# A unit's row of maxima: one write, loads right behind it, and no extra maxima in the first four cycles of an attention kernel

## The chip, the cores and the metric

The kernel runs on one core of a Trainium2 chip. The metric is the device time of one execution in microseconds. Before the change three runs took 1613.4, 1613.86 and 1617.51 us: the median is 1613.86.

## What is computed

One block of a transformer with adaptive layer norm, in float32: 2048 tokens, width 512, 32 query heads of width 16 that share one key head and one value head, and a dense layer of width 1792 with ReLU.

```python
mod = (silu(c) @ w_mod).reshape(1, 6, 1, 512)
sa, ca, ga, sb, cb, gb = (mod[:, i] for i in range(6))
h = layernorm(x) * (1 + ca) + sa
q = (h @ wq).reshape(1, 2048, 32, 16).transpose(0, 2, 1, 3)
k, v = h @ wk, h @ wv
p = softmax(einsum("bhqd,bkd->bhqk", q, k) * 16 ** -0.5)
x = x + ga * (merge_heads(einsum("bhqk,bkd->bhqd", p, v)) @ wo)
h = layernorm(x) * (1 + cb) + sb
return x + gb * (relu(h @ w1) @ w2)
```

## The kernel before

**Units.** The attention is cut into 32 units: 8 blocks of 256 tokens times 4 groups of 8 heads. A unit has its queries in two tiles `qp`, four columns (`ct` 0 to 3) of 512 query rows each, two in the lower half of the partitions and two in the upper. Rows 0 to 47 of a half hold the queries, split in a high and a low part so that a product of rounded numbers keeps its precision; rows 48 and 49 hold minus the row maximum, high and low part, against rows of ones in the keys `kp`. So a score matmul (`scores`, TensorE, line 907) gives the score less its maximum, and the exponential (ScalarE, line 909) needs no further work. `values` (line 1084) multiplies the exponentials `pe` with the values into the bank `ps_pv`.

**Row of maxima.** Before that, `max_of` computes the same products (line 534, into one of three banks `ps_max`) and VectorE reduces each to its maxima (line 536), 64 times a unit. After the last, VectorE reduces once more (`negm`, line 540) and transposes (`sq`, line 496). `max_rows` returns two steps. `parts` splits `sq` into `ms`, high part on ScalarE (line 314), low part on GpSimd (line 315), and writes it to a scratch tensor `mdr` in DRAM. `load` reads `mdr` back as rows 48 and 49 of the unit's `qp`, in four loads, one for each `ct`. A write or load waits on its queue until what it needs is done, and what stands behind it in that queue waits too. For unit 0 both use SP's and ScalarE's queue, later only SP's.

**Cycles.** The main loop has 256 cycles, 8 for each unit. In a cycle go 8 score matmuls with their exponentials, 8 maxima of the next unit (a "place"), two groups of value matmuls, and a portion of other matmuls into the one bank `ps_fill`, the fill: query projections in cycles 0 to 32 and a few later ones, then the output projection and the dense layer of the block that is done. A string of letters sets the order in a cycle; there is one for each size of the portion. `a` and `b` are maxima, `c` and `d` scores, `u` and `l` fill matmuls on the upper and lower half of TensorE's rows, `V` the value matmuls, `P` the place where steps of ScalarE and GpSimd that were put off are issued. Work on the lower half of the rows runs beside work on the upper half, so the letters come in pairs.

```python
    6: "aucuaucPeuaucuasdVtbldlbldldelblbscV",
    3: "bcaucuuacdlbldlbVPbacddaV",
    "e": "aucuaucPeuaucuadVtbldlbldldelblbcV",
```

A portion of three matmuls has the order 3, which holds its maxima in pieces of five and three. The order 6 has four in each half. Portions of six, and the first ones in full float32, use it. The letter `e` is an extra maximum of a list `extra`. It holds the 8 maxima of one place, which go two to a cycle in the cycles 0 to 3. With the 16 maxima of unit 1 that are done before the loop, a unit's last maximum falls three places ahead: unit u's maxima end in cycle 8u - 4, and its first scores, which run one or two ahead of their cycle, stand late in cycle 8u - 1.

**The row in the loop.** Its `parts` goes to the end of the list `put_off` in cycle 8u - 3 and is issued at that cycle's `P`. Its `load` goes to `ends`, which is issued at the end of the same cycle. `put_off` also holds the splits of other tiles (`hh`, `r`, `w1s`, `qq`), and `to_dram`, three stores of 256 KB that bring a projected query tile to DRAM (`qdr`, line 429). `load_q` reads such a tile back for the next unit (line 480), 16 maxima before the unit's end. From cycle 13 on, with pauses, chores are issued at a cycle's end: loads of weights (`raw`, lines 862 and 873) and stores of their split form (`w1dr`, line 868). In the dense layer SP loads `w1s` (line 562), one tile of 512 KB a cycle.

Of the kernel before, what the change touches and what calls it, by code (L numbers as in the profile page):

```python
# [9 lines left out]
F32 = mybir.dt.float32  # L10
# [19 lines left out]
KB = S // 512  # L30
# [37 lines left out]
def build(tc, nc, cst, sb, ps, dr, x, wq, wk, wv, wo, w1, w2, c, w_mod, out):  # L68
# [244 lines left out]
    def split(hi, lo, src, eng=None):  # L313
        nc.scalar.activation(hi, src, AF.Copy)  # L314
        (eng or nc.gpsimd).tensor_tensor(lo, src, hi.bitcast(F32), op=OP.subtract)  # L315
# [4 lines left out]
    def split_psum(hi, lo, pt, func=AF.Copy, stg=None, **kw):  # L320
        stg = stage() if stg is None else stg
        nc.scalar.activation(stg, pt, func, **kw)  # L322

        def parts():
            split(hi, lo, stg)

        return parts


    put_off = []  # L330

    def add_psum(dst, pt, other):
        stg = stage()
# [84 lines left out]
    def qproj(b, j, bank, soon=False, tag=None, n0=0):  # L418


        pt = bank()
        todo = [("f32", pt[:, n:n + TB], wqf[j][:, k], hT[b][:, k, n:n + TB],
                 n + k == n0, n + k == TB + DC - 1)
                for n in range(n0, LB, TB) for k in range(DC)]

        def to_dram(qq):
            stored.add((b, j))
            for r, part in ((0, 0), (32, 0), (16, 1)):
                nc.sync.dma_start(qdr[b][j].bitcast(F32)[:, r:r + 16, n0:], qq[:, part, n0:].bitcast(F32))

        def end():
            qt = sb.tile([P, 2, LB], F32R, name="qq", tag=tag or "t4", bufs=3 if tag else 2)
            if soon:
                nc.scalar.activation(qt[:, 0, n0:], pt[:, n0:], AF.Copy, scale=DH ** -0.5)
                nc.vector.scalar_tensor_tensor(qt[:, 1, n0:], pt[:, n0:], DH ** -0.5,
                                               qt[:, 0, n0:].bitcast(F32),
                                               op0=OP.mult, op1=OP.subtract)
                to_dram(qt)
                return
            stg = sb.tile([P, 512], F32, name="stg", tag="tmp", bufs=2)  # L440
            put_off.append(split_psum(qt[:, 0, n0:], qt[:, 1, n0:], pt[:, n0:], stg=stg[:, n0:], scale=DH ** -0.5))
            put_off.append(partial(to_dram, qt))

        return todo, end

# [46 lines left out]
    def max_rows(u, negm):  # L492


        sq = sb.tile([P, 32], F32, name="sq", tag="sq", bufs=2)
        nc.vector.transpose(sq, negm)
        mdr = dr.tile([2, 16, 4, 32], F32, name="mdr", tag="mdr", bufs=4)

        def queue(n):
            return nc.scalar if u == 0 and n % 2 else nc.sync  # L500

        def parts():
            ms = sb.tile([P, 2, 32], F32R, name="ms", tag="ms", bufs=2)
            split(ms[:, 0], ms[:, 1], sq)
            for q in range(4):
                queue(q).dma_start(mdr[:, :, q].rearrange("p a n -> a p n"),
                                   ms[q * 32:q * 32 + 16].bitcast(F32))

        def load():
            for ct in range(4):  # L510
                r = (ct % 2) * 64 + 48
                queue(ct).dma_start(qps[u][ct // 2][r:r + 2].bitcast(F32),
                                    mdr[:, ct * 4:ct * 4 + 4].rearrange("p j q n -> p (j q n)"))

        return parts, load

# [27 lines left out]
    places = [(0, i, j) for i in range(2) for j in range(4)]  # L544
    first_max = [(0, hf, i, j, kb) for kb in range(KB) for _, i, j in places for hf in (1, 0)]
    places = [(u, i, j) for u in range(1, NU) for _, i, j in places]
    first_max += [(u, hf, i, j, kb) for u, i, j in places[:LEAD // 8]
                  for kb in range(KB) for hf in (1, 0)]
    places = places[LEAD // 8:]
    extra = [(*places[0][:1], hf, *places[0][1:], kb) for kb in range(KB) for hf in (1, 0)]  # L550
    places = places[1:]

# [485 lines left out]
    for what in HEAD:  # L1040
        if what == "q":
            q = firsts.pop(0)
# [25 lines left out]
    pvt, ends = None, []  # L1068
# [5 lines left out]
    def in_turn(steps):  # L1074
        for step in steps:
            step()
# [13 lines left out]
    for c in range(NU * KT // 2):  # L1090
# [4 lines left out]
        if places:  # L1095
            u, i, j = places.pop(0)
# [2 lines left out]
        todo_of["e"] = [partial(max_of, *m) for m in extra[:2]]  # L1099
        del extra[:2]  # L1100
        for parts, load in later:
            put_off.append(parts)
            ends.append((c, load))
        later.clear()
        halves = [in_two(turn) for turn in turns]
        turns.clear()
# [9 lines left out]
        todo_of["V"] = [partial(values, s + n) for n in range(2)]  # L1116
        for what in order:
            if what == "P":
                in_turn(put_off)
                put_off.clear()  # L1120
            elif what == "p":
                in_turn(put_off[:1])
                del put_off[:1]
            elif what == "s":
                if fine:
                    step = fine.pop(0)
                    if step:
                        step()
            elif todo_of.get(what):
                todo_of[what].pop(0)()  # L1130
# [43 lines left out]
```

## Time and profile before

| | |
|---|---|
| median of three runs | 1613.86 us |
| the profiled execution | 1613.94 us |
| its span | 1612.0 us |
| busy: TensorE, VectorE, ScalarE, GpSimd | 99%, 83%, 77%, 21% of the span |
| the chain that ended last | 97% TensorE |
| 16 DMA engines, mean busy share of queue 1 | 24.9% |

The span runs from the first to the last instruction of the profiled execution; the execution is 1.94 us longer. The program's first 82 us (layer norm, keys, values, the first queries and unit 0's maxima) come ahead of the loop. The first value matmul of cycle 0 starts at 85.97 us. In rows of the profile, PE stands for TensorE, PEld for its weight loads, DVE for VectorE, ACT for ScalarE, POOL for GpSimd, SPq and ACTq for the DMA queues of SP and ScalarE. A row in order of time has the start, the length, the engine, the line, the operation, the tile written and read, and in brackets how long the engine was idle and what ended that.

### The profile page before, as it was taken

What the parts mean: (1) busy time and instruction counts of PE and PEld (TensorE: products, weight loads), DVE (VectorE), ACT (ScalarE), POOL (GpSimd) and SP (SyncE); (2) the same over time, 40 slices, a digit from 0 to 9 for tenths busy, and PEclk for the clock granted to TensorE, in tenths of its full rate; (3) what the DMA queues carried; (4) which work ended last, traced back from release to release, by engine and by line L of the source; (5) the groups of instructions that cost most, each with busy time, mean ns of one, the idle gap of its engine ahead of it and who ended that gap; (6) DMA issues with size and microseconds to landing.
All of it is one profiled execution on the core that took longest, in us unless ns stands there. A gap on an engine that the chain in (4) does not pass through costs nothing.

```text
span 1612.0 us, 33902 instructions
## 1 busy us (share of the span) xinstructions
PE 1602.8 (99%) x13036; PEld 926.5 (57%) x13036; DVE 1337.6 (83%) x2296; ACT 1237.7 (77%) x2447; POOL 336.9 (21%) x391
## 2 busy tenths in 40 slices
PE   9999999999999999999999999999999999999999
PEld 6444445556555665556655565556655565556668
DVE  7999998988889888988889888988889888987031
ACT  5279898888887887778877887778877887778831
POOL 5023332335511210121111210121111210121110
PEclk9999999999999999999999999999999999999999
DMA  7111343445211330213111330213211230103241
GB/s 263 57 40 56 102 150 114 133 156 170 83 41 39 102 96 4 63 48 108 56 36 43 89 96 17 62 34 110 69 37 43 67 106 29 61 17 106 71 169 57
DMA packets 87665, 129.10 MB, mean 80 GB/s; under 512 B 25093, under 2 KB 52677, under 8 KB 87505
## 3 DMA queue, kind: packets, MB, share of 16 engines
q1 hardware_dynamic: 85688, 126.78, 24.9%
q8 instruction: 104, 1.70, 0.4%
q14 instruction: 57, 0.46, 0.1%
q10 hardware_dynamic: 1816, 0.15, 0.1%
HBM read 99.94 MB, written 24.76 MB: 77 GB/s over the span
## 4 chain that ended last, share of the span: by engine, by line
PE 97%; DVE 1%; DMA 1%; ACT 0%; issue 0%; ACTq 0%; POOL 0%; DVEq 0%
PE ps_pv L1084 32%; PE ps_max L534 22%; PE ps_fill L202 21%; PE ps_exp L907 16%; PE ps_max L185 2%; PE ps_exp L185 1%; DVE pm L536 1%; PE ps_exp L394 1%; PE ps_fill L185 1%; DMA wmod<-in_w_mod_dram 1%; PE ps_max L198 0%; PE ps_exp L369 0%; PE ps_exp L466 0%; DMA ccol<-in_c_dram 0%; DMA mdr<-ms 0%; PE ps_pv L466 0%
## 5 line engine op out<-in xcount | busy, mean ns | idle before, releaser
L536 DVE TENSOR_REDUCE pm<-ps_max 128x1 f32<-128x512 f32 x2028 | 1259.2, 682 | 154.2 <-PE ps_fill L202 107.7
L909 ACT ACTIVATE pe<-ps_exp 128x512 f32<-128x512 f32 x2048 | 1079.7, 606 | 256.6 <-PE ps_fill L202 165.2
L534 PE MATMUL ps_max<-kp,qp 48*128 48x512 f32 x2028 | 796.0, 423 | 1.3 <-DMA qp<-qdr 0.7
L907 PE MATMUL ps_exp<-qp,kp 50*128 50x512 f32 x2048 | 737.0, 403 | 0.5 <-ACT pe L909 0.4
L534 PEld LDWEIGHTS ps_max<-kp,qp 48*128 48x128 f32 x2028 | 366.6, 185 | 444.5 <-DVE pm L536 413.8
L1084 PE MATMUL ps_pv<-pe,vt 128*32 128x512 f32 x4096 | 545.5, 605 | 0.0
L907 PEld LDWEIGHTS ps_exp<-qp,kp 50*128 50x128 f32 x2048 | 376.0, 186 | 26.6 <-ACT pe L909 12.2
L202 PE MATMUL ps_fill<-w2r,r 64*128 64x512 f32 x1044 | 288.0, 408 | 0.0
L202 PE MATMUL ps_fill<-hh,w1s 64*128 64x256 f32 x1568 | 237.7, 291 | 0.0
L202 PEld LDWEIGHTS ps_fill<-hh,w1s 64*128 64x128 f32 x1568 | 196.8, 185 | 13.5 <-issue 10.1
L202 PEld LDWEIGHTS ps_fill<-w2r,r 64*128 64x128 f32 x1044 | 179.6, 185 | 19.4 <-issue 4.2
L1084 PEld LDWEIGHTS ps_pv<-pe,vt 128*32 128x32 f32 x4096 | 80.6, 108 | 130.1 <-issue 122.2
L202 PE MATMUL ps_fill<-hl,w1s 64*128 64x256 f32 x784 | 124.7, 279 | 0.0
L315 POOL TENSOR_TENSOR r<-stg,r 128x512 fp32r<-128x512 f32 x49 | 63.0, 1285 | 285.6 <-ACT r L314 278.6
L202 PEld LDWEIGHTS ps_fill<-hl,w1s 64*128 64x128 f32 x784 | 106.1, 185 | 0.0
L1133 POOL TENSOR_TENSOR on<-num,den 128x256 f32<-128x256 f32 x31 | 23.1, 746 | 170.0 <-DMA den<-recs 121.3
L322 ACT ACTIVATE stg<-ps_fill 128x512 f32<-128x512 f32 (+1 forms) x64 | 39.4, 616 | 4.8 <-PE ps_fill L185 4.8
L936 POOL COPY num<-pvs 128x256 f32<-128x256 f32 x31 | 12.4, 399 | 134.7 <-ACT pvs L919 100.5
L202 PE MATMUL ps_fill<-wol,oh 64*128 64x512 f32 x112 | 38.0, 418 | 0.0
L315 POOL TENSOR_TENSOR ol<-on,oh 128x512 fp32r<-128x512 f32 x14 | 18.0, 1286 | 91.7 <-ACT oh L314 86.1
L335 POOL TENSOR_TENSOR x<-stg,x 128x512 f32<-128x512 f32 x14 | 18.1, 1292 | 85.3 <-ACT stg L334 85.3
L202 PE MATMUL ps_fill<-woh,oh 64*128 64x512 f32 x112 | 33.5, 418 | 0.0
(200 smaller groups left out, 1003.4 us busy)
## 6 DMA issues: line engine op xcount, KB each, us to landing
w1s<-w1dr SPq DMA_DIRECT2D x104, 512.0 KB
qp<-qdr SPq DMA_DIRECT2D x124, 96.0 KB
qdr<-qq SPq DMA_DIRECT2D x45, 256.0 KB
raw<-in_B_w_dram SPq DMA_DIRECT2D x28, 256.0 KB
w1dr<-w1s SPq DMA_DIRECT2D x14, 512.0 KB
wmod<-in_w_mod_dram SPq DMA_DIRECT2D x6, 1024.0 KB
x<-in_A_x_dram SPq DMA_DIRECT2D x8, 512.0 KB
out_dram<-ot SPq DMA_DIRECT2D x16, 256.0 KB
```

The costliest lines, as they stand in the source:

```text
L185: nc.tensor.matmul(pt, w, a, start=start, stop=stop)
L202: ins = nc.tensor.matmul(pt, w[r], a[r], start=start and h == 1, stop=stop and h == 0)
L315: (eng or nc.gpsimd).tensor_tensor(lo, src, hi.bitcast(F32), op=OP.subtract)
L322: nc.scalar.activation(stg, pt, func, **kw)
L335: nc.gpsimd.tensor_tensor(dst, stg, other, op=OP.add)
L394: nc.tensor.matmul(pt, wkv[:, k * P:(k + 1) * P], hT[b][:, k], start=k == 0, stop=k == DC - 1)
L534: nc.tensor.matmul(pt, qps[u][i][r, j * P:(j + 1) * P], kp[r, kb * 512:(kb + 1) * 512], start=True, stop=True)
L536: nc.vector.tensor_reduce(pms[u][:, (i * 2 + hf) * 4 + j, kb:kb + 1], pt, axis=AX.X, op=OP.max)
L907: nc.tensor.matmul(pt, kp[r, kt * P:(kt + 1) * P], qps[u][ct // 2][r], start=True, stop=True)
L909: nc.scalar.activation(pe, pt, AF.Exp)
L1084: nc.tensor.matmul(pvt[i * 32:(i + 1) * 32], vt[:, kt], pes.pop((s, i)), start=(kt == 0), stop=(kt == KT - 1))
L1133: due[1]()
```

## The change

Five things change. `extra` is empty, and its place stays in the list of places: unit u's maxima end in cycle 8u - 3 and its row is made in cycle 8u - 2. `mdr` has another layout, so that one DMA of 128 pieces of 256 bytes writes it (before: four DMAs of 32 pieces of 128 bytes). The loads read 32 pieces of 128 bytes each (before: 2 pieces of 2 KB). In the loop `parts` and `load` are put at the head of `put_off`, one behind the other, or at its end in a cycle whose list holds `modulate_two`. The query stores go to a list `stores`, issued behind `put_off` at the same `P`.

```diff
-    put_off = []
+    put_off, stores = [], []
...
-            put_off.append(partial(to_dram, qt))
+            stores.append(partial(to_dram, qt))
...
-        mdr = dr.tile([2, 16, 4, 32], F32, name="mdr", tag="mdr", bufs=4)
+        mdr = dr.tile([32, 4, 2, 32], F32, name="mdr", tag="mdr", bufs=4)
...
-            for q in range(4):
-                queue(q).dma_start(mdr[:, :, q].rearrange("p a n -> a p n"),
-                                   ms[q * 32:q * 32 + 16].bitcast(F32))
+            nc.sync.dma_start(mdr.rearrange("a q p n -> q a (p n)"),
+                              ms.rearrange("p r n -> p (r n)").bitcast(F32))
...
-                                    mdr[:, ct * 4:ct * 4 + 4].rearrange("p j q n -> p (j q n)"))
+                                    mdr[ct * 4:ct * 4 + 4].rearrange("j q p n -> p (j q) n"))
...
-    extra = [(*places[0][:1], hf, *places[0][1:], kb) for kb in range(KB) for hf in (1, 0)]
-    places = places[1:]
+    extra = []
...
         for parts, load in later:
-            put_off.append(parts)
-            ends.append((c, load))
+            turned_now = any(getattr(f, "func", None) is modulate_two for f in put_off)
+            at = len(put_off) if turned_now else 0
+            put_off[at:at] = parts, load
...
             if what == "P":
-                in_turn(put_off)
+                in_turn(put_off + stores)
                 put_off.clear()
+                stores.clear()
```

Lines of the changed kernel are one or two lower than before from line 534 on (534 is 533, 907 is 905, 1084 is 1082).

TensorE's order in the second half of a cycle among the first four, from one group of value matmuls to the next. Before:

```order
L1084 MATMUL ps_pv<-pe,vt 32x512 x4
L534 MATMUL ps_max<-kp,qp 128x512
L907 MATMUL ps_exp<-qp,kp 128x512
L534 MATMUL ps_max<-kp,qp 128x512
L202 MATMUL ps_fill<-hT,wq_84 128x256
L907 MATMUL ps_exp<-qp,kp 128x512 x2
L534 MATMUL ps_max<-kp,qp 128x512 x2
L202 MATMUL ps_fill<-hT,wq_84 128x256
L534 MATMUL ps_max<-kp,qp 128x512
L907 MATMUL ps_exp<-qp,kp 128x512
L1084 MATMUL ps_pv<-pe,vt 32x512 x4
```

And now:

```order
L1082 MATMUL ps_pv<-pe,vt 32x512 x4
L533 MATMUL ps_max<-kp,qp 128x512
L905 MATMUL ps_exp<-qp,kp 128x512
L533 MATMUL ps_max<-kp,qp 128x512
L202 MATMUL ps_fill<-hT,wq_84 128x256
L905 MATMUL ps_exp<-qp,kp 128x512 x2
L533 MATMUL ps_max<-kp,qp 128x512
L202 MATMUL ps_fill<-hT,wq_84 128x256
L533 MATMUL ps_max<-kp,qp 128x512
L905 MATMUL ps_exp<-qp,kp 128x512
L1082 MATMUL ps_pv<-pe,vt 32x512 x4
```

Four maxima stand there in place of five.

SP's queue around the row of unit 3, in cycles 21 to 23 (`mdr<-ms` writes the row, `qp<-mdr` loads it, `qdr<-qq` are query stores, `w1dr` and `raw` chores). Before:

```order
L868 DMA w1dr_111<-w1s 128x1024
L862 DMA raw<-in_B_w_dram 128x4x128
L506 DMA mdr<-ms 16x2x32 x4
L429 DMA qdr_3_132<-qq 8x16x512 x3
L512 DMA qp<-mdr 2x512 x4
L868 DMA w1dr_112<-w1s 128x1024
L862 DMA raw<-in_B_w_dram 128x4x128
```

And now:

```order
L866 DMA w1dr_111<-w1s 128x1024
L860 DMA raw<-in_B_w_dram 128x4x128
L429 DMA qdr_3_132<-qq 8x16x512 x3
L866 DMA w1dr_112<-w1s 128x1024
L860 DMA raw<-in_B_w_dram 128x4x128
L505 DMA mdr<-ms 4x32x64
L511 DMA qp<-mdr 2x16x32 x4
```

The row moved behind the query stores of cycle 21 and the chores of that cycle's end; its loads moved up to its write.

ScalarE's order ahead of the loop, around the row of unit 0 (`mrow` and `gr` are copies of products that TensorE goes on with). Before:

```order
L314 ACTIVATE ms<-sq 128x32
L506 DMA mdr<-ms 16x2x32 x2
L512 DMA qp<-mdr 2x512 x2
L413 ACTIVATE vt<-ps_exp 128x4x16
L228 ACTIVATE mrow<-ps_exp 128x512
```

And now:

```order
L314 ACTIVATE ms<-sq 128x32
L511 DMA qp<-mdr 2x16x32 x2
L413 ACTIVATE vt<-ps_exp 128x4x16
L228 ACTIVATE mrow<-ps_exp 128x512
L245 ACTIVATE gr<-ps_fill 128x512
```

The two writes on ScalarE's queue are gone; its two loads still wait for the row's write.

## The prediction

> **What bounds the kernel now.** I read the page first (span, busy times, the chain that ended last, the costliest group), then cut the span into stretches, then read single engines in order of time at the places that the change touches. The page:
>
> ```profile
> span 1612.0 us, 33902 instructions
> ...
> PE 1602.8 (99%) x13036; PEld 926.5 (57%) x13036; DVE 1337.6 (83%) x2296; ACT 1237.7 (77%) x2447; POOL 336.9 (21%) x391
> ...
> PE 97%; DVE 1%; DMA 1%; ACT 0%; issue 0%; ACTq 0%; POOL 0%; DVEq 0%
> ...
> L536 DVE TENSOR_REDUCE pm<-ps_max 128x1 f32<-128x512 f32 x2028 | 1259.2, 682 | 154.2 <-PE ps_fill L202 107.7
> ```
>
> TensorE is busy all the time and carries the chain, so only what shortens or stretches its cycles counts. The change takes no matmul away. But a TensorE that waits for a PSUM bank between two groups of matmuls still reads as busy here, so the length of a cycle has to be taken from stretches. The columns below are the stretch, its length, and the busy time of PE, PEld, DVE, ACT and POOL with their instructions:
>
> ```profile
> core 0: us, PE busy (x) PEld busy (x) DVE busy (x) ACT busy (x) POOL busy (x), PEclk, DMA share, GB/s
> 85.97:112.03 26.06, 25.99 (x180) 12.46 (x178) 24.19 (x41) 19.51 (x39) 5.82 (x5) 1.00 0.15 45
> 112.03:117.70 5.67, 5.67 (x46) 3.20 (x44) 5.17 (x11) 4.63 (x11) 1.29 (x1) 1.00 0.28 81
> 244.30:247.44 3.14, 3.09 (x24) 1.42 (x22) 3.00 (x7) 2.61 (x6) 0.50 (x1) 1.00 0.00 0
> 1474.50:1480.20 5.70, 5.70 (x58) 3.53 (x56) 4.90 (x9) 4.64 (x10) 1.52 (x2) 1.00 0.32 109
> 1485.90:1491.60 5.70, 5.70 (x50) 3.51 (x48) 0.00 (x0) 4.80 (x12) 1.49 (x2) 1.00 0.14 30
> ```
>
> The first row is four cycles from middle to middle, three and a half of them with the extra maxima: 6.5 us each, VectorE busy 24.19 of 26.06. The second is the next cycle, without them: 5.67. The last two are a late cycle with eight maxima and one with none: both 5.70.
>
> **The extra maxima of the first four cycles.** VectorE in order of time, two halves of cycles with an extra maximum, then one without, then the end of unit 1's row:
>
> ```profile
> 90.82 3.08 DVE L536 TENSOR_REDUCE pm<-ps_max 128x1 f32<-128x512 f32 x5 [0.23 <-PE ps_max L534]
> 94.12 3.08 DVE L536 TENSOR_REDUCE pm<-ps_max 128x1 f32<-128x512 f32 x5 [0.23 <-PE ps_max L534]
> ...
> 113.55 2.49 DVE L536 TENSOR_REDUCE pm<-ps_max 128x1 f32<-128x512 f32 x4 [0.36 <-PE ps_max L534]
> 116.14 0.22 DVE L540 TENSOR_REDUCE negm<-pm 128x16 f32<-128x64 f32 x1
> ```
>
> With five maxima a half lasts 3.30 us (94.12 - 90.82): 3.08 of reductions and 0.23 of waiting. With four it lasts 2.49 + 0.36 = 2.85. Four cycles from middle to middle hold seven halves with an extra maximum: 26.06 - 4 x 5.67 = 3.4 us. The eighth, the first half of cycle 0, starts with VectorE behind by what the start has left, and ScalarE late too; I give it 0.1 of the 0.45 (bounds 0 and 0.45). ScalarE needs 19.51 / 4 = 4.9 us a cycle there, so it does not take VectorE's place at 5.67. **Term: -3.5 us** (-3.4 to -3.9). The eight maxima reappear in a cycle near 1486, which has none now. There the fill matmuls alone set 5.70, with maxima or without: 0.
>
> **The row of unit 0.** It is written by SP and ScalarE's queue together, two each, and now by SP in one. ScalarE's queue keeps two loads:
>
> ```profile
> 72.01 1.99 ACTq L506 DMA_DIRECT2D mdr<-ms  x2
> 75.34 0.77 ACTq L512 DMA_DIRECT2D qp<-mdr  x2
> ...
> 76.91 0.42 PEld L251 LDWEIGHTS ps_exp<-idn,mrow 128*128 128x128 f32 x4 [1.19 <-ACT mrow L228]
> 77.50 0.28 PEld L534 LDWEIGHTS ps_max<-kp,qp 48*128 48x128 f32 x1 [0.17 <-DVE pm L536]
> 78.22 0.71 PEld L251 LDWEIGHTS ps_exp<-idn,mrow 128*128 128x128 f32 x4 [0.44 <-ACT mrow L228]
> ```
>
> ScalarE cannot go on before its loads have been issued at 76.1, and TensorE waits for it at 76.91 and 78.22. With one write, whose landing 1.42 us after issue stands in the next fence, the loads go out near 73.5 instead of 75.34. The first wait brings little, because the maxima at 77.50 wait for VectorE, which is not earlier; the second goes. **Term: -0.45 us** (0 to -1.2).
>
> **The row of every other unit.** It ends one cycle later (the extra place is done in turn), is split first in its cycle, is written once, and its loads follow at once, ahead of the query stores. It removes three DMA issues a unit, which cost only SP's time. What decides is whether the loads land before the first scores of the unit, since these now come one cycle sooner behind the row. SP in order of time, for units 1, 3 and 4, and a write and a load of 128 pieces of 64 bytes elsewhere:
>
> ```profile
> 119.83 1.71 SPq L506 DMA_DIRECT2D mdr<-ms  x4
> 122.55 1.13 SPq L512 DMA_DIRECT2D qp<-mdr  x4
> ...
> 207.35 1.72 SPq L506 DMA_DIRECT2D mdr<-ms  x4
> 209.16 1.90 SPq L429 DMA_DIRECT2D qdr<-qq  x3
> 211.25 2.77 SPq L512 DMA_DIRECT2D qp<-mdr  x4
> ...
> 247.69 1.94 SPq L429 DMA_DIRECT2D qdr<-qq  x3
> 250.52 2.92 SPq L506 DMA_DIRECT2D mdr<-ms  x4
> 257.69 1.13 SPq L512 DMA_DIRECT2D qp<-mdr  x4
> ...
> 642.05 0.34 SPq L949 DMA_DIRECT2D recs<-rc  x1
> 643.47 0.65 SPq L950 DMA_DIRECT2D den<-recs  x1
> ...
> 1507.42 0.34 SPq L945 DMA_DIRECT2D rc<-sums  x1
> ...
> 1510.14 0.25 DVE L948 RECIPROCAL rc<-rc 128x16 f32<-128x16 f32 x1 [25.19 <-DMA rc<-sums]
> ```
>
> No row shows the merged write or a load in 32 pieces of 128 bytes. A write in small pieces lands within 643.47 - 642.05 = 1.42 us, a load in small pieces within 1510.14 - 1507.42 = 2.7 us. I take these for the new ones; the lower bound of a load is 1.4, as for a write. What is in the queue ahead costs more: unit 1's write and loads are 2.7 us apart (122.55 - 119.83), unit 4's, behind three query stores, 7.2 (257.69 - 250.52). The Trainium skill (DMA: Bandwidth & Descriptors, section Queues, rings and completion order) has each DMA engine take descriptors in ring order; the trace agrees with 7.2 against 2.7. If that order did not bind, the next term would be 0 and the sum 1609.8.
>
> TensorE at the first scores of unit 3, with a cycle of the same kind ahead of it for comparison:
>
> ```profile
> 123.91 1.06 PE L1084 MATMUL ps_pv<-pe,vt 128*32 128x512 f32 x8
> 125.25 0.63 PE L907 MATMUL ps_exp<-qp,kp 50*128 50x512 f32 x3
> 125.82 1.06 PE L1084 MATMUL ps_pv<-pe,vt 128*32 128x512 f32 x8
> ...
> 214.91 1.07 PE L1084 MATMUL ps_pv<-pe,vt 128*32 128x512 f32 x8
> 216.39 1.00 PE L907 MATMUL ps_exp<-qp,kp 50*128 50x512 f32 x3
> 217.35 1.06 PE L1084 MATMUL ps_pv<-pe,vt 128*32 128x512 f32 x8
> ```
>
> This piece lasts 2.44 us in place of 1.91: unit 3's loads, issued behind the stores, are already late by 0.5. After the change the stores stay in their cycle and go out up to 1.8 us sooner (the writes ahead of them are gone), so they end about 7 us after 207.4, at 214.4. The chores of that cycle (a 512 KB store and a 256 KB load, now ahead of the row) follow; between 0 and 4 us, I take 1. Then the row's write ends near 215.4, its four loads are issued until 216.6 and land between 218.0 and 219.3. They are needed at 216.2. So unit 3 loses 1.8 to 3.1 us where it lost 0.5 (and gains 0.5 if the chores cost nothing and the write slips in). Half of such a stall comes back, as VectorE, which sets these cycles, keeps its backlog of maxima. **Term: +1.0 us** (-0.5 to +3). Unit 2 has the same with one 256 KB load: +0.2 (0 to +1.5). Unit 1 has nothing ahead; written at 125.1 it has landed by 125.1 + 1.4 + 1.1 + 2.7 = 130.3, when the scores come at 129.2 + 1.3 = 130.5: 0.
>
> VectorE's closing reduction and transposition (116.14, 0.43 us together) move a cycle too. Unit 1's leaves a half whose wait of 0.36 hid it for one where VectorE is full: +0.1 (0 to +0.4). Unit 4's leaves the half from 244.30, which took 3.14, for one of 2.85: -0.25 (-0.3 to 0). Units 2 and 3 stay among full cycles, later ones among cycles that TensorE sets: 0.
>
> **Sum:** -3.5 - 0.45 + 1.0 + 0.2 + 0.1 - 0.25 = -2.9 us. Against the profiled execution's 1613.94 (its span of 1612.0 and 1.94 around it) that is 1611.0; the median of the runs is 1613.86, so it is 1611.0 there too, 0.18% less. About 0.3% (4.8 us) is what a measurement of this kernel can tell from no change.
>
> **Rivals.** First, the rows land in time. The stall of 0.5 goes, and the sum is -3.5 - 0.45 - 0.5 - 0.15 = -4.6 us: 1609.3; with the other ends of the first two terms -5.8: 1608.1. For it: in units 2 and 3 the row is put ahead of the stores of its own cycle; against it, the stores of the cycle before are still there. Second, the start gives nothing back: cycles 0 to 3 keep 6.2 us or the late rows of units 2 and 3 cost all of it; 1613.5. Against: the second stretch has the same order of work at 5.67.
>
> Third, slower: the loads in small pieces land late for every unit of the long even part. One unit there:
>
> ```profile
> 938.32 1.72 SPq L506 DMA_DIRECT2D mdr<-ms  x4
> 941.05 1.13 SPq L512 DMA_DIRECT2D qp<-mdr  x4
> ...
> 949.45 0.39 PE L907 MATMUL ps_exp<-qp,kp 50*128 50x512 f32 x1
> ```
>
> The score at 949.45 is the first that needs the row. A cycle later, the write goes out at 944.0 and the last load lands by 944.0 + 1.4 + 1.1 + 2.7 = 949.2. So the slack can be down to 0.2 us; the split now first in its cycle adds some. From there each 1 us later costs 27 units 1 us each: 1638, and 0.3 us is enough to be slower than before. The Trainium skill (the same page, section Specifications) asks for at least 512 bytes a piece and has smaller ones done as read and write again; it speaks for this rival. The 64-byte load of 2.7 us speaks against it, as the bound above has it in.
>
> **Chances.** Forecast, with part of the gain given back: 0.53, between 1609.5 and 1612.8. Rows in time: 0.28, of which 0.2 is faster than 1609.0. Nothing won: 0.14. Late everywhere: 0.05. So faster 0.2, same 0.75, slower 0.05. The range takes in the first rival's end and the second: 1608.1 to 1613.9.
>
> **What would show it.** In the profile after: the stretch of the first four cycles near 22.7 us with VectorE busy for about 20; TensorE's wait for ScalarE near 78 gone; the cycle near 1486 with eight maxima and still 5.7; and the first scores of units 2 and 3 late by up to 2 us behind their loads, with all later units not waiting. Wrong would be: halves of cycles 0 to 3 above 3.0 us, or the cycles of the even part no longer at 5.7.

## The result and the profile after

The changed kernel took 1616.55 us (median of 22 runs, 1614.12 to 1621.49), the kernel before 1614.14 us beside it (22 runs, 1612.08 to 1617.57). The ratio is 1.0014 (95% interval 1.0008 to 1.002): the change made the kernel slower, by 2.4 us. 1611.0 had been predicted, with 1608.1 to 1613.9 as the range. One execution below, of run 7, took 1893 us at a mean clock of 0.751 and is left out. The profiled execution took 1618.01 us, its span 4.2 us more than before:

```profile
span 1616.2 us, 33824 instructions
...
PE 1603.6 (99%) x13036; PEld 928.3 (57%) x13036; DVE 1338.6 (83%) x2296; ACT 1238.6 (77%) x2447; POOL 337.6 (21%) x391
...
PE 92%; DMA 3%; issue 2%; DVE 1%; POOL 1%; SPq 0%; ACT 0%; POOLq 0%
```

The page has changed little (DMA has 3% of the chain that ended last in place of 1%), so the stretches have to tell. Columns as in the prediction; the first row is the first four cycles, the second the next cycle, the third to fifth the cycles around unit 3's first scores, the last a cycle that has maxima now and had none:

```profile
core 0: us, PE busy (x) PEld busy (x) DVE busy (x) ACT busy (x) POOL busy (x), PEclk, DMA share, GB/s
83.39:106.28 22.89, 22.89 (x171) 12.93 (x170) 19.69 (x33) 19.25 (x40) 5.84 (x5) 1.00 0.15 45
106.28:111.96 5.68, 5.68 (x47) 3.31 (x45) 4.96 (x9) 4.64 (x11) 1.29 (x1) 1.00 0.34 105
...
210.02:215.67 5.65, 3.31 (x16) 1.14 (x15) 2.54 (x5) 2.41 (x5) 1.26 (x1) 0.85 0.30 101
215.67:221.15 5.48, 5.48 (x27) 2.54 (x25) 3.21 (x5) 3.47 (x7) 0.40 (x1) 0.53 0.24 64
221.15:226.60 5.45, 5.45 (x44) 2.61 (x46) 4.73 (x9) 4.58 (x11) 1.29 (x1) 1.00 0.34 108
...
1489.46:1495.15 5.69, 5.69 (x53) 3.51 (x52) 4.02 (x8) 4.83 (x12) 1.29 (x1) 1.00 0.29 92
```

The first four cycles fell from 26.06 to 22.89, with VectorE at 19.69. The last row shows the eight maxima back for nothing: 5.69 against 5.70. The third and the fourth row are new. In 210.02 to 215.67 TensorE was busy for 3.31 of 5.65 us, and in the next stretch it was busy throughout, but at a granted clock of 0.53.

To find every place that changed I took the start of each group of value matmuls, which come twice a cycle, and compared the time from one to the next before and after. Such a half is named by the cycle in which it starts. These are the halves that differ by more than 0.1 us, after less before, without two pairs that cancel to 0.03 (cycles 12 and 13, 20 and 21: the closing reductions of units 2 and 3):

| place | half of a cycle, before to after | difference, us |
|---|---|---|
| first value matmul of cycle 0 | 85.97 to 83.39 | -2.58 |
| cycles 0 to 3, seven halves | 3.30 to 2.84, the last to 2.98 | -3.15 |
| unit 2's first scores (cycle 15) | 1.89 to 2.83, the next 3.63 to 3.48 | +0.79 |
| unit 3's first scores (cycle 23) | 2.43 to 5.65, the next 3.42 to 5.48 | +5.27 |
| unit 4's closing reduction (cycles 28, 29) | 3.14 to 2.84, 2.83 to 2.98 | -0.15 |
| unit 4's first scores (cycle 31) | 2.98 to 3.77 | +0.79 |
| cycle 35 | 2.92 to 3.24 | +0.32 |
| cycles 46 to 50, four halves | 2.99 to 3.12, 2.84 to 3.38, 2.90 to 3.66, 2.86 to 3.56 | +2.12 |
| the 205 cycles behind (four halves by -0.26 to +0.29) | | -0.1 |
| behind the last group | 66.74 to 67.56 | +0.8 |

The rows come to 4.1, and the rest of the 4.2 lies in smaller differences. The extra maxima and the start together gave 5.7 us, unit 3 alone took 5.3 back, three smaller stalls took 3.7, and the long even part did not move. Not all of this is in every execution, and the medians differ by 2.4 us, not 4.2: in runs 7 and 11 below, whose edits concern unit 3 alone, unit 4's half lost nothing and 0.23, and cycles 46 to 50 lost 1.5 and 1.2. The half of cycle 35 is longer than before in all other kernels, run 1 included, by 0.2 to 0.7 us, and that is not explained.

**Unit 3.** SP's queue and TensorE, in order of time:

```profile
201.42 2.66 SPq L429 DMA_DIRECT2D qdr<-qq  x3
204.13 0.59 SPq L866 DMA_DIRECT2D w1dr<-w1s  x1
204.77 0.83 SPq L860 DMA_DIRECT2D raw<-in_B_w_dram  x1
205.77 2.23 SPq L505 DMA_DIRECT2D mdr<-ms  x1
212.20 1.21 SPq L511 DMA_DIRECT2D qp<-mdr  x4
```

```profile
210.02 1.07 PE L1082 MATMUL ps_pv<-pe,vt 128*32 128x512 f32 x8
211.02 0.49 PE L533 MATMUL ps_max<-kp,qp 48*128 48x512 f32 x2
213.78 1.93 PE L905 MATMUL ps_exp<-qp,kp 50*128 50x512 f32 x3 [2.27 <-DMA qp<-mdr]
215.67 1.93 PE L1082 MATMUL ps_pv<-pe,vt 128*32 128x512 f32 x8
```

The write of 32 KB, issued at 205.77, had not landed until 212.19, 6.4 us later, behind three stores (the last landed at 209.72), `w1dr` (210.96) and `raw` (211.72). The loads could not be issued before 212.20, and TensorE waited 2.27 us. Behind that wait eight value matmuls took 1.93 us in place of 1.07: the granted clock was 0.50 from 214.02 to 220.85 us.

**Cycles 46 to 50.** SP's queue after, then before:

```profile
349.48 0.53 SPq L505 DMA_DIRECT2D mdr<-ms  x1
351.83 1.22 SPq L511 DMA_DIRECT2D qp<-mdr  x4
353.09 1.84 SPq L429 DMA_DIRECT2D qdr<-qq  x3
355.29 6.78 SPq L560 DMA_DIRECT2D w1s<-w1dr  x2
362.17 2.46 SPq L936 DMA_DIRECT2D num<-pvs  x4
```

```profile
345.79 2.69 SPq L429 DMA_DIRECT2D qdr<-qq  x3
352.78 0.85 SPq L562 DMA_DIRECT2D w1s<-w1dr  x2
355.61 2.73 SPq L938 DMA_DIRECT2D num<-pvs  x4
```

Cycle 46 is the one in which unit 6's row meets both `modulate_two`, so that the row goes to the end of `put_off`, and query stores, which now stand behind it. While SP waits for the row's split and for its write, the stores and what follows wait too: `num` left at 362.17 in place of 355.61, in an execution whose cycle 46 starts 1.4 us later.

**The start.** ScalarE issues its two loads at 74.09 in place of 75.34, and the waits of TensorE's weight loads for `mrow`, 1.19 and 0.44 us before, have shrunk to one of 0.24. Only behind the first did the matmuls stand idle too, for 0.88 us:

```profile
76.92 0.65 PE L251 MATMUL ps_exp<-idn,mrow 128*128 128x128 f32 x4 [0.88 <-ACT mrow L228]
```

There is more in the 2.6 us than that. Before, the profiled execution had this stretch:

```profile
77.51:80.92 3.41, 3.41 (x11) 2.20 (x10) 1.99 (x6) 0.33 (x1) 0.00 (x0) 0.50 0.00 0
```

It ran 3.41 us at half the clock; after, the clock was 1.00 there.

**Runs and the clock.** The mean granted clock goes with the time of a run. Of 88 runs of the kernel before, taken beside the experiments, 63 had a mean of 0.999 or more (median 1613.35), 14 had 0.997 to 0.998 (1614.27) and 11 less (1616.63). Of the 22 of the changed kernel 2 had 1.000 (1614.12 and 1614.20), 14 had 0.997 to 0.998 (1616.39) and 6 less (1619.19). So nearly every run of the changed kernel lost clock somewhere. Where, the mean does not tell; the profiles with unit 3's wait (after, runs 4, 7 and 10) all have the 6.83 us at 0.50 there. The two without a loss of clock were 2.2 us faster than the 14.

### The profile page after: what moved, and what is told of

Its sections match the earlier page's. It is cut to its first block, busy times and chain, and to the rows that moved or that the text cites. A ratio compares the mean times of both kernels' runs of the same rounds, so it can differ in the third digit from the quotient of the medians.

```text
span 1616.2 us, 33824 instructions
## 1 busy us (share of the span) xinstructions
PE 1603.6 (99%) x13036; PEld 928.3 (57%) x13036; DVE 1338.6 (83%) x2296; ACT 1238.6 (77%) x2447; POOL 337.6 (21%) x391
## 4 chain that ended last, share of the span: by engine, by line
PE 92%; DMA 3%; issue 2%; DVE 1%; POOL 1%; SPq 0%; ACT 0%; POOLq 0%
PE ps_pv L1082 30%; PE ps_max L533 20%; PE ps_fill L202 20%; PE ps_exp L905 15%; PE ps_max L185 2%; PE ps_exp L185 1%; PE ps_exp L394 1%; PE ps_fill L185 1%; DMA mdr<-ms 1%; DVE pm L535 1%; DMA qdr<-qq 1%; DMA wmod<-in_w_mod_dram 1%; PE ps_exp L369 0%; PE ps_max L198 0%; DMA qp<-qdr 0%
```

## The experiments

My theory was that the rows of units 2, 3 and 4 land late because of the DMA work ahead of them, and that TensorE's wait then costs more than its length through the clock. The rival was that the new layout is slow: small pieces, or a single write. "Half" means the time between two groups of value matmuls, as in the table.

**1. The layout alone** (`e1_layout`). The kernel before with the new `mdr`, its one write and its loads; the row's place, the stores and the extra maxima as before.

```diff
-        mdr = dr.tile([2, 16, 4, 32], F32, name="mdr", tag="mdr", bufs=4)
+        mdr = dr.tile([32, 4, 2, 32], F32, name="mdr", tag="mdr", bufs=4)
...
+            nc.sync.dma_start(mdr.rearrange("a q p n -> q a (p n)"),
+                              ms.rearrange("p r n -> p (r n)").bitcast(F32))
```

> The kernel before with one edit: the row is written in one DMA in the new layout and read in pieces of 128 bytes; extra maxima, the place of the row in its cycle and the loads at the cycle's end stay. Late-row theory (the loss comes from which cycle the row stands in and what is in the queue ahead of it): only the start changes, first scores near 80.4 us in place of 82.6, and no first score of a unit waits longer than before; 2.4 us faster than before, 1611.7. Small-piece rival (reads of 128 bytes land late): units 1 to 4 wait at their first scores as in the changed kernel, 3 us or more slower than before, 1617.

Measured: 1612.99 us, ratio 0.9997 (0.9989 to 1.0006). The loads in pieces of 128 bytes landed 1.52 us after issue (median of the units behind 500 us), those of 2 KB before 1.44. The start came 2.4 us earlier than in the profile of before, but most of that is the clock (run 10), and the median gained 0.8 where I had expected 2.4. Unit 3's half went from 2.43 to 1.88: with one write in place of four its row was in time. New was a wait of 0.94 us at the first maxima of unit 2, for its queries: the four loads took SP 2.86 us to issue in place of 1.75. I did not find why. The layout is not what made the kernel slower.

**2. The extra maxima back** (`e2_extra_back`). The changed kernel with the list `extra` of before.

```diff
-    extra = []
+    extra = [(*places[0][:1], hf, *places[0][1:], kb) for kb in range(KB) for hf in (1, 0)]
+    places = places[1:]
```

> The changed kernel with the extra maxima of the first four cycles back, so that every unit's row is made one cycle earlier; one write, split first, loads ahead of the stores stay. Late-row theory: cycles 0 to 3 take 6.6 us again (3.2 us more than the changed kernel), the stall of unit 3 (2.4 us of waiting and 2.9 us at a lower clock) and that of cycles 47 to 50 (2.0 us) are gone; first scores near 80.4; 2.5 to 3 us faster than before, 1611.3. Small-piece rival: the stalls stay, 3 us slower than the changed kernel.

Measured: 1612.84 us, ratio 1.0002 (0.9993 to 1.0012); seven of its 12 runs, those with a mean clock of 0.999 or more, lie at 1611.8 to 1612.9. Unit 3's half is 1.88, and those of cycles 46 to 50 are as before. So all these stalls come with the later row; the new place alone costs nothing but the wait for unit 2's queries that run 1 has too (0.86 here). The profiled execution (1617.47) had a granted clock of 0.50 from 64.34 to 81.40 us, ahead of the loop; a loss of that size, in 5 of the 12 runs by their mean clock, is what its interval is wide from.

**3. No chore ahead of unit 3's row** (`e3_pause21`).

```diff
-        if c >= 13 and not 24 <= c < 28 and not 31 <= c < 36:
+        if c >= 13 and c != 21 and not 24 <= c < 28 and not 31 <= c < 36:
```

> The changed kernel without the chore at the end of cycle 21 (a 512 KB store and a 256 KB load, which come one chore step later; all later chores shift by one step), so that the row of unit 3 has only the query stores ahead of it. Late-row theory: the row's write of unit 3 lands about 2 us sooner, the wait at its first scores falls from 2.3 us to under 1 us and the lower clock behind it goes; 4 to 5 us faster than the changed kernel, 1611.8 to 1612.5. Small-piece rival: the wait stays above 2 us and so does the lower clock; no change against the changed kernel, 1616.5.

Measured: 1610.0 us, ratio 0.9979 (0.997 to 0.9987): 6.5 us less than the changed kernel, and faster than before. SP's queue and TensorE at the same place:

```profile
201.10 2.67 SPq L429 DMA_DIRECT2D qdr<-qq  x3
205.45 0.53 SPq L505 DMA_DIRECT2D mdr<-ms  x1
208.21 1.21 SPq L511 DMA_DIRECT2D qp<-mdr  x4
```

```profile
209.74 1.06 PE L1082 MATMUL ps_pv<-pe,vt 128*32 128x512 f32 x8
211.07 0.62 PE L905 MATMUL ps_exp<-qp,kp 50*128 50x512 f32 x3
211.62 1.06 PE L1082 MATMUL ps_pv<-pe,vt 128*32 128x512 f32 x8
```

The loads go out 4 us earlier with the same three stores ahead, the half is 1.88, and the loop has no stretch at half clock. The 768 KB of that cycle's chores were the difference between in time and 3 us late.

**4. The row always first in its cycle** (`e4_front_always`). This was to mend cycle 46.

```diff
-            at = len(put_off) if turned_now else 0
+            at = 0
```

> The changed kernel with the row put at the head of the list in every cycle, also in those whose list holds the modulation of the dense layer's input. In cycle 46 the row's write then goes out some 2.5 us sooner, and with it the query stores and the loads of dense weights behind it. Held-queue theory: the extra 2.0 us of cycles 47 to 50 fall to 1 us or less, the other stalls stay; 1 to 2 us faster than the changed kernel, 1614.5 to 1615.5. Rival (the dense weights are late for another reason): cycles 47 to 50 as in the changed kernel, and up to 0.3 us more in each of the blocks' cycles 13 to 15, as the split behind it is later; 1616.5 to 1618.

Measured: 1625.49 us, ratio 1.0073 (1.0061 to 1.0085), above both ranges. The halves of cycles 47, 48 and 50 went back, but cycle 46 lost 3.2 us, and one half in every 32 cycles (78, 110, to 238) 1.28 us. Near cycle 78:

```profile
532.35 0.25 POOL L315 TENSOR_TENSOR ms<-sq,ms 128x32 fp32r<-128x32 f32 x1 [4.28 <-ACT ms L314]
532.58 1.09 POOL L601 TENSOR_SCALAR stg<-stg,cols 128x256 f32<-128x256 f32 x2
```

```profile
533.70 0.63 ACT L314 ACTIVATE hh<-stg 128x512 fp32r<-128x512 f32 x1 [1.44 <-POOL stg L601]
```

The row's split on GpSimd waits for VectorE's transposition, `modulate_two` stands behind it, and ScalarE, which needs its result for `hh`, holds its exponentials for 1.44 us. So the end of the list in such a cycle is the right place for the row, as the changed kernel has it.

**5. More pauses, stores ahead of the row in cycle 46** (`e5_paused_46`). `last` is the row's first step where the row went to the end of `put_off`.

```diff
-                in_turn(put_off + stores)
+                at = put_off.index(last) if last else len(put_off)
+                in_turn(put_off[:at] + stores + put_off[at:])
...
-        if c >= 13 and not 24 <= c < 28 and not 31 <= c < 36:
+        if c >= 14 and c not in (21, 29) and not 24 <= c < 28 and not 31 <= c < 36:
```

> The changed kernel with chores started at cycle 14 and paused in 21 and 29 (nothing of them ahead of the rows of units 2, 3 and 4), and in a cycle whose row stands at the end of put_off the query stores go ahead of that row. Theory (what stands ahead of a row in SP's queue makes it late, and in cycle 46 the row made the stores and loads behind it late): the halves of cycles 15, 23 and 31 go back to 1.9, 1.9 and 3.0 us, and those of 47, 48 and 50 to 2.85 or a part of the way there, since the row's write now waits for the stores' data; against 1610.0 of the kernel with the pause in 21 alone that is -0.7 - 0.6 - 0.5 to -2.0, so 1606.7 to 1608.2. Rival (rows are late in 15 and 31 because they are made a cycle later, whatever stands ahead): the halves of 15 and 31 keep 2.8 and 3.6, and the time is 1609.5 to 1610.

Measured: 1619.05 us, ratio 1.0034 (1.0023 to 1.0046): a miss. The halves of cycles 15, 23 and 31 did go to 1.89, 1.89 and 2.98, which answers the rival for 15. For 31 it does not: unit 4's half is at 2.98 in runs 4, 7 and 12 too, with chores ahead of its row. The write landed 4.1 to 4.8 us after its issue there and 5.5 after it in the changed kernel, so this stall stands on the edge, and its cause stays open. But cycles 44 and 45 lost 2.9 us and 46 lost 6.5. The chores ended three cycles later, and two causes were mixed; run 8 parts them.

**6. The empty list alone** (`e6_extra_only`). The kernel before with `extra = []` and nothing else.

> The kernel before with the empty list of extra maxima alone: four writes, large loads, loads at the cycle's end, row at the end of put_off. Theory (lateness comes from the row being made a cycle later behind stores and chores, not from its pieces): cycles 0 to 3 give 3.15 us as in the changed kernel; unit 3's loads go out at the end of cycle 22, later than in the changed kernel, so cycles 23 and 24 lose 5 to 8 us, with the granted clock down to about 0.5 behind the wait; units 2 and 4 lose 1 to 2 each. 1613.8 - 3.15 + 7 to 12: 1617.6 to 1622.6, and the even part, whose loads would land about 0.1 us ahead of the first scores, adds 0 to 1 us for each of 26 units. Rival (the new layout and the new place of the loads made the rows late): -3.15 and no stall, 1610.7.

Measured: 1651.5 us, ratio 1.0236 (1.0219 to 1.0254), far above what I expected. Units 2 and 3 lost 3.0 and 3.7 us, but unit 1 lost 7.9, unit 5 3.2, unit 6 7.3, and of the even part every fourth unit 1.9 to 3.7, none of which I had expected. The first scores of the unit near 560 us, SP's queue and TensorE:

```profile
557.66 0.36 SPq L664 DMA_DIRECT2D out_dram<-ot  x1
558.06 0.43 SPq L561 DMA_DIRECT2D w1s<-w1dr  x1
558.67 1.15 SPq L512 DMA_DIRECT2D qp<-mdr  x4
```

```profile
561.70 0.48 PE L906 MATMUL ps_exp<-qp,kp 50*128 50x512 f32 x1 [1.55 <-DMA qp<-mdr]
```

At a cycle's end the loads stand behind a store of results and a load of 512 KB. I had them land just in time there, with nothing ahead of them. So the change's other parts are worth 35 us once the list is empty. It is also the clearest view of the clock. Unit 1's first scores waited 4.25 us, until 131.38:

```profile
126.00:128.96 2.96, 1.13 (x10) 0.19 (x2) 2.19 (x4) 0.92 (x2) 1.26 (x1) 1.00 0.37 126
128.96:139.20 10.24, 7.65 (x32) 3.51 (x36) 3.55 (x6) 5.06 (x10) 0.40 (x1) 0.50 0.03 9
139.20:142.00 2.80, 2.80 (x24) 0.75 (x16) 1.95 (x4) 1.74 (x4) 1.29 (x1) 1.00 0.04 9
```

The clock stays at 0.50 for 10.24 us, 7.8 of them after the wait has ended.

**7. Unit 3's write on ScalarE's queue** (`e7_write_act`). Is it the order in SP's queue that holds the write, or the work of the DMA engines?

```diff
-            nc.sync.dma_start(mdr.rearrange("a q p n -> q a (p n)"),
+            (nc.scalar if u == 3 else nc.sync).dma_start(mdr.rearrange("a q p n -> q a (p n)"),
```

> The changed kernel with unit 3's write, and only that one, issued on ScalarE's queue. Its loads stay on SP's. Theory (the write waits in the order of SP's queue behind three stores, w1dr and raw): it lands by about 208.5 us in place of 212.2, the loads are issued at once and land behind raw near 212.5 to 213, and unit 3 loses 0 to 1.5 us in place of 5.3, with the granted clock at 1.00 behind it: 1611.0 to 1612.8. Rival (the DMA engines are busy with these 1.5 MB whichever queue asks): the write lands near 212 here too, unit 3 loses 5 us, 1616 to 1617.

Measured: 1615.21 us (median of 11), ratio 1.0012 (1.0001 to 1.0022). The rival was right about the write and the stall; the time is 0.8 us under its range:

```profile
208.73 0.77 SPq L860 DMA_DIRECT2D raw<-in_B_w_dram  x1
```

```profile
209.72 0.65 ACTq L505 DMA_DIRECT2D mdr<-ms  x1
```

```profile
216.36 1.21 SPq L511 DMA_DIRECT2D qp<-mdr  x4
```

This execution runs 3.9 us later there than that of the changed kernel, so the write was issued at the same point. On the other queue it landed at 216.34, 6.6 us after its issue and 0.5 after `raw` (215.88), and TensorE waited 2.30 us. This small write landed behind all that had been issued before it, on either queue.

The Trainium skill (DMA: Bandwidth & Descriptors, section Queues, rings and completion order) states that a DMA engine goes round its queues packet by packet, and that the step which reports a transfer done lands only after every earlier write of that engine, across its queues. The 6.6 us agree with the second and leave nothing to be seen of the first.

**8 and 9. Chores moved, and the one order in cycle 46** (`e8_chores_moved`, `e9_row_ahead_46`). Run 8 is run 5 with chores in cycles 27 and 35 as well; run 9 is run 8 without the edit of `in_turn`.

```diff
-        if c >= 14 and c not in (21, 29) and not 24 <= c < 28 and not 31 <= c < 36:
+        if c >= 14 and c not in (21, 29) and not 24 <= c < 27 and not 31 <= c < 35:
```

> As the kernel before it with chores paused in 13, 21 and 29 and the stores ahead of the row in cycle 46, but the chores go on in cycles 27 and 35 too, so that they end one cycle later than in the changed kernel and not three. Theory (that kernel lost its 9 us at cycles 44 to 46 because the split weights were not yet stored when the dense layer came to load them; the rest is the DMA work ahead of the rows): the halves of 44 to 46 go back to about 3.1, 3.1 and 3.0, those of 15, 23 and 31 stay at 1.9, 1.9 and 3.0, no stretch with a granted clock of 0.50 in the loop, and the time is 1606.5 to 1608.5. Rival (the stores ahead of the row made that loss): 46 and 47 lose 3 to 9 us here too, 1611 to 1617.

> As the kernel beside it, with the row ahead of the query stores in cycle 46, as in the changed kernel: the one difference is the order of nine transfers on SP's queue in that cycle. Theory (the row's wait holds back the stores, and the next loads of weights wait for a tile that the stores free): the halves of 47, 48 and 50 keep 3.3, 3.2 and 3.6, 1.2 us more than beside it, 1607.7 to 1609.7. Rival (these halves are late because of the row's own lateness): the same in both kernels, within 0.4 us.

Measured: 1614.61 us (ratio 1.0006, 0.9996 to 1.0015) and 1610.36 us (0.9977, 0.9967 to 0.9987). Cycles 44 and 45 are as before in both, so run 5's loss there came from late chores. The order of the row's five transfers and the three stores in cycle 46 is worth 4.2 us, to the other side than I thought; run 8's rival was right that the stores ahead of the row cost time, in cycle 47. In run 8:

```profile
339.95 2.69 SPq L429 DMA_DIRECT2D qdr<-qq  x3
342.75 0.52 SPq L505 DMA_DIRECT2D mdr<-ms  x1
347.63 1.22 SPq L511 DMA_DIRECT2D qp<-mdr  x4
```

The write takes 4.9 us behind the stores, TensorE waits 2.67 us for the loads, the clock is 0.50 for 6.8 us, and cycle 47 loses 5.9. The halves of 48 and 50 are as before in run 8 and keep 3.42 and 3.65 in run 9: so it is the stores held back by the row that cost 1.3 us there, as I had said (47, for which I had said it too, is as before in run 9). But that is the cheaper of the two orders.

**10. The old pieces at the new place** (`e10_old_pieces`). The changed kernel with the old layout, its four writes and its loads of 2 KB pieces.

> The changed kernel with the old scratch layout: four writes of 32 pieces of 128 bytes and loads of 2 pieces of 2 KB, at the new place and without the extra maxima. Theory (the place of the loads is what makes an empty extra list possible, the pieces are worth little): the write takes 0.6 us longer to land, units 10, 14, 18, 22, 26 and 30, whose loads have 0.3 to 0.5 us to spare in the changed kernel, lose 0 to 0.4 us each, the others, with 2 us, nothing; unit 3 loses 5 to 6 as in the changed kernel. With the start as before (0 to 2.4 us more): 1616.5 to 1621. Rival (the one write does it): late by 2 to 5 us in every second or third unit, as in the kernel with the empty list alone, 1635 or more.

Measured: 1620.64 us, ratio 1.0041 (1.0028 to 1.0055), within the theory's range. Units 2 and 4 lose 0.3 and 0.1 us more than in the changed kernel, unit 3 as much (5.1), one unit of the even part 1.2. Of the 35 us between run 6 and the changed kernel the new place gives 31 by the medians. The layout's 4 rest on four executions; the profiled ones account for 1.0 of them. In this execution the first value matmul comes at 83.95 with no loss of clock, in that of the changed kernel at 83.39: the layout's part of the start is 0.55 us, not 2.6.

**11. TensorE kept busy in unit 3's wait** (`e11_busy_wait`).

```diff
+        if u == 3 and 3 not in filled:
+            filled.add(3)
+            spare = next(max_banks)()
+            for _ in range(9):
+                nc.tensor.matmul(spare, qps[3][0][:48, :P], kp[:48, :512], start=True, stop=True)
```

> The changed kernel with nine extra products (48 x 512 columns, into a bank of ps_max that nobody reads) on TensorE just ahead of unit 3's first scores, where it waits 2.27 us for the row. They add 2 us of work inside the wait and need nothing of the row. Theory (the granted clock is halved for 3.4 or 6.8 us because TensorE idles there, and that is 2 us of the stall's price): TensorE's wait shrinks to 0.3 us, the granted clock stays at 1.00 behind it, the halves of cycle 23 and 24 are 4.8 and 3.8 in place of 5.65 and 5.48, and most executions take 1614.0 to 1614.8, as the two of the changed kernel whose mean clock was 1.000. Rival (the clock falls for another reason, or the price is the wait alone): the stretch of 0.50 stays and the time is 1616 to 1617, or, if the products are not covered, 1618.

The profiled execution did what the theory says:

```profile
211.41 2.33 PE L910 MATMUL ps_max<-kp,qp 48*128 48x512 f32 x9
213.58 1.36 PE L912 MATMUL ps_exp<-qp,kp 50*128 50x512 f32 x3
214.90 1.07 PE L1089 MATMUL ps_pv<-pe,vt 128*32 128x512 f32 x8
```

The scores start as late as before (213.58 against 213.78), the value matmuls take 1.07 us, the clock is 1.00 throughout, and the two halves are 4.83 and 3.41 in place of 5.65 and 5.48: 2.9 us less for nine products more, and 1613.44 us. The timing does not bear it out: 1615.85 us, ratio 1.0017 (1.0006 to 1.0028), the same as the changed kernel's. Five of its 11 runs, two with a mean clock of 1.000 and three with 0.998, took 1613.4 to 1614.5, where the changed kernel had two of 22; the other six had less clock and took 1615.9 to 1620.3. Where they lost it no profile tells. So that the wait lowers the clock is seen at this place in one execution with the wait filled, against four profiles with the wait (after, runs 4, 7 and 10); that filling it speeds the kernel up is not shown.

**12. Unit 2 cleared** (`e12_unit2_clear`). One pause fewer than run 9.

```diff
-        if c >= 13 and not 24 <= c < 28 and not 31 <= c < 36:
+        if c >= 14 and c != 21 and not 24 <= c < 27 and not 31 <= c < 36:
```

> The changed kernel with no chore at the end of cycles 13 and 21 and one more in cycle 27, so that the chores end one cycle later. Theory (DMA work ahead of a row makes it late): the stalls of units 2 and 3 go, those of unit 4 (0.6) and of cycles 47 to 50 (1 to 1.5) stay, and the time is 0.7 us under that of the kernel with the pause in 21 alone: 1608.8 to 1610.0. Rival (what is gained in one place is lost by other transfers, as in the kernel that paused 29 as well): 1610 to 1611.

Measured: 1609.95 us, ratio 0.9982 (0.9972 to 0.9991). It lies where the two ranges meet. Unit 2's halves are back at 1.90 and 3.63 and, which I had not expected, unit 4's at 2.98 (as in runs 4 and 7), yet the time is that of run 3, as is run 9's. Against run 3 the profile shows 0.8 us gone elsewhere, in cycles 35, 142 and 149, and 0.3 behind the last group. That is the size by which these places differ between other kernels here too, and I cannot tell it from chance. Three kernels, 3, 9 and 12, beat both, by 3.5 to 3.8 us against the one before; none beats the others.

## Why the prediction was wrong, point by point

- **Extra maxima, -3.5.** Right: -3.15 (run 6 has the same in another kernel). The halves are 2.84 where 2.85 was worked out, and the maxima near 1486 cost nothing.
- **The row of unit 0, -0.45.** About right for the layout (0.55, run 10), by two readings that were not: the one write landed after 2.1 us and not after 1.42, so that the loads went out at 74.09 and not near 73.5, and the 0.44 us at 78.22 that were to go were of weight loads, while the matmuls ran on. That the wait of 0.88 us there is followed by 3.4 us of half clock I did not see. In most runs of before this loss was not there, so the median gained less than the profile.
- **Unit 3, +1.0.** This is the step that failed: 5.3 us. The way there was nearly right: I had the stores end, the chores behind them, and the loads 1.8 to 3.1 us late, and they were 2.3 to 3.4 late; the chores cost 2.0 us and not the 1 that I chose from "0 to 4". What was wrong is that "Half of such a stall comes back". Little did: the half behind the stall took 3.41 us (run 11) where it takes 3.64 without one (run 3). Without loss of clock (run 11) the two halves lost 2.4 us against before, and the clock added 2.9. A stall of TensorE has to be priced above its length here, not below it.
- **Units 2 and 4.** +0.2 became +0.8. Unit 4 I had only as a gain of 0.25 by its closing reduction (it was 0.15) and not as late, though the prediction's own rows show its row behind three stores and a wait of 7.2 us: I looked for what was new ahead of the row and not for how much sooner it was needed. It is +0.8 in the profile, but 0 to 0.6 in runs 3, 4, 7, 11 and 12, which leave its row alone.
- **Unit 1's closing reduction, +0.1.** Not found: no half from cycle 4 to 8 differs by 0.1.
- **Cycles 46 to 50.** Not in the sum: +2.1 in the profile. I read what the new place does to the row, and in that one cycle not what the row does to the stores and loads behind it. The prediction had asked only whether rows land in time.
- **The even part, 0.** Right. In the changed kernel the last load lands about 2.4 us ahead of the first score in most units and 0.3 to 1.0 in every fourth; the prediction's bound of 0.2 was near for those and too tight for the rest.
- **Behind the last group, +0.8.** Not foreseen and not explained. It is 66.7 in the kernels with the old layout (before, runs 6 and 10) and 66.9 to 67.6 in the others. No run was made for it.
- **Rivals.** "Late everywhere from small pieces" falls (run 1). "Rows in time" is what run 3 made true for unit 3: 1610.0, against 1609.3 worked out for it. That the totals are so near is in part luck, since units 2 and 4 and cycles 46 to 50 still lost 3.0 us in run 3's profile. A stall in one unit that eats the gain was in the range only up to 3 us.

The Trainium skill's rule on ring order that the prediction set beside its trace held, and further than within a ring (run 7). The Trainium skill's rule on pieces of at least 512 bytes, which the prediction set beside its third rival, would have spoken for slow loads; 128-byte pieces took 0.1 us more than 2 KB ones (run 1).

## What to carry to other kernels

Before a transfer is moved next to its need, add up the bytes issued ahead of it on all queues and how much sooner it is needed, unit by unit, and then ask what the engine that waits for it holds back behind itself. Price a wait of the engine that bounds the kernel at its full length, and where it is TensorE add what the half clock behind it may take: here 2.9 us for a stretch of 6.83. Compare one profiled execution with another only after the stretches of granted clock in both have been laid side by side.

## What the runs showed of the hardware

The granted clock fell to 0.50 in stretches of 3.41, 6.83, 10.24, 13.65 or 17.07 us, whole multiples of 3.413 us, but for the one that the end of each profile cuts off. In one profile they all start on one grid with that step. Windows of this grid that lie just ahead of such a stretch, at full clock themselves:

| profile | window, us | TensorE busy in it, us | half clock behind it, us |
|---|---|---|---|
| before | 74.10 to 77.51 | 2.43 | 3.41 |
| run 6 | 559.04 to 562.45 | 1.86 | 3.41 |
| run 6, unit 1 | 125.55 to 128.96 | 1.58 | 10.24 |
| run 8 | 345.45 to 348.86 | 1.35 | 6.83 |
| after | 210.61 to 214.02 | 1.14 | 6.83 |
| run 6 | 367.89 to 371.30 | 0.00 | 6.83 |

From 60 us to the last group of value matmuls the 14 profiles have 21 windows at full clock in which TensorE was busy for 2.45 us or less. Half clock followed behind 18 of them: for two windows behind the seven with less than 1.4 us, for one behind ten with 1.7 us or more, and for three in unit 1 of run 6, where TensorE waited on into the first of them. Behind three with 2.16 to 2.27 us (runs 5 and 6) it did not. Behind windows with 2.47 us or more it did so twice, ahead of the loop in single executions (13.65 us in run 7, 17.07 in run 2), where I found no cause. The waits of 0.75 us that came back every 32 cycles in run 4 left 2.6 us of work in their windows and did not lower the clock. So what counts here is not a wait's length alone but how much of one window it takes. Two of 22 runs of the changed kernel lost no clock, by their mean; no profile shows one of them.

The Trainium skill (TensorE: Matmul & The Clock Gate, section The HAM clock gate) gives a free-running window of 3413 ns, half rate behind an idle one and full rate behind a busy one. The lengths and the grid agree; the full rate behind a busy one does not always: in run 10 TensorE was busy for all 3.41 us from 215.59 at half clock, and the next window was at half clock too. A rule of the Trainium skill on the same page (section Why this matters for your kernels) is to avoid gaps above about 3 us; here waits of 2.27 us (after) and 0.88 us (before) were enough.
